# Pooled attention and two gated layers on one core: values pooled by head pairs in the first batch, a new plan of the first steps, and a denominator formed as a product with h

## The chip, the cores and the metric

The kernel runs on one core of a Trainium2 chip. The metric is device time in microseconds (us) of one launch, the median of several runs. Beside the runs stands one profiled execution, from which all rows below are taken. Engine names in rows: PE is TensorE (matmul), PEld its weight load, DVE is VectorE, ACT is ScalarE, POOL is GpSimd, SP is SyncE, which issues all DMAs of this kernel (SPq is its queue).

## The reference

```python
k_p = k.reshape(B, H, S//8, 8, D).mean(axis=3)       # B=8, H=8, S=576, D=64: 72 pooled keys
v_p = v.reshape(B, H, S//8, 8, D).mean(axis=3)
attn = softmax(scale * q @ k_p^T)                    # scale = 1/8
x = (attn @ v_p) as (4608, 512)                      # tokens x (head, d)
h = x @ w_in                                         # 512 -> 2048
P = a0 + a1*h + a2*h^2 + a3*h^3
Q = 1 + |b0|*|h| + |b1|*h^2
x = (P / (Q + 1e-6)) @ w_out                         # 2048 -> 512
out = (sigmoid(x @ w_gate) * (x @ w_val)) @ w_out2   # 512 -> 1536 -> 512
```

All of it is in 32-bit floats. The kernel splits both operands of each large product into a high and a low part, so that one product is three matmuls (`mm3`, L472).

## The kernel before

**Tiling.** The 4608 tokens are cut at the borders of batches and of 128 tokens into 40 attention tiles of 128 or 64 tokens (`token_tiles`). A block of the first layer has 512 tokens; there are nine, and each goes through 16 slices of 128 of the 2048 hidden features: 144 steps n. The four tiles of block 0 belong to batch 0; a fifth, of 64 tokens, ends that batch and opens block 1. The second layer runs after step 143, in six pairs of 384-token blocks; the change doesn't touch it.

**A step n** (loop at L759). `g1` makes h for one slice of features in a PSUM bank. `rational1`, `rational2` and `rational3` (L510 to L533) make P/Q of it: ScalarE forms Square, a scaled Abs and an affine from h, VectorE the sum u = |b1|·h² + |b0|·|h| (L517, from two SBUF tiles) and the cubic (L518, L519 with h from PSUM), ScalarE then Ln(1 + u) and Exp(-ln), the reciprocal, and VectorE corrects it and multiplies (L531 to L533). `split_g` splits the result of the step before; `g2` multiplies with w_out three steps later (LAG). In steps 0 to 15 `weights_a` also loads w_in and w_out and splits them, on ScalarE (L92, L94, L117), VectorE (L100, L118) and GpSimd (L102, L118).

**Attention** is spread over the steps by a plan (L429 to L465): a list of pieces with a step, a rank within it, and a part (0 before `split_g`, 2 behind `rational2`, 1 behind `g2`), one part for TensorE's half and one for the rest. For a tile: scores and subtraction of the maximum (L347 to L365), exponential (L371), normalisation (L378 to L382, the product on GpSimd), transposes (L389, copied by ScalarE at L393), attend (L404, copied into xs at L409 and L410). Steps -8 to -1 are the prologue (L744), in which only attention and weight conversion run; step 0 needs all of xs of block 0.

**Keys and values.** A batch's keys are pooled on VectorE in five chunks (L314) and put into a block-diagonal tile (L323). Its values come as five chunks of 128 rows (head, pooled position), are pooled on GpSimd (L331, L332) into `vp`, and 12 small DMAs (`heads_v`, L344) move them into `vh`, where the 72 pooled positions of each head start at partition 0, as the attend needs them. Batch b+1 is pooled during the steps of batch b; for batch 1 that is step -2 (keys), -1 and 0 (values).

**Order.** Each engine runs its instructions in the order of the program. Loads are issued by SyncE in the order of the plan (`units`): the first 14 into tiles that are free at the start (`early`), then three into a ring (`raw_p`), whose refill is issued when a pooling has read its slot (`done`). Five more go into named tiles in step -7.

## Time and profile before

| | us |
|---|---|
| runs, median of 3 (lowest to highest) | 1831.88 (1828.98 to 1833.6) |
| profiled execution | 1829.29 |
| its span, first to last instruction | 1827.1 |

One step of the rational in the middle of the first layer takes about 6.4 us (816.60 us for 127 steps between 173.4 and 990 us). A row of the timeline gives the start and the duration of one group of equal instructions, and in brackets the idle time of the engine ahead of it and what ended that. A table of waits gives who waited for whom: total, times, longest. TensorE's busy time is modelled at its ends, and some matmul records can be missing.

### The profile page before, as it was taken

To read this page: it belongs to the slowest core of one execution; us is meant where nothing else is said; L and a number is where in the kernel's file an instruction comes from. 1 tells how busy PE (TensorE), PEld (TensorE's weight loads), DVE (VectorE), ACT (ScalarE), POOL (GpSimd) and SP (SyncE) were. 2 spreads that over 40 slices of the span, in tenths; PEclk is the share of its full clock that TensorE was granted. 3 is DMA by queue.
4 is the path that set the end of the run, shared out by engine and by line. 5 is a ranking of instruction groups with operands and counts; after the bars stand their busy time and mean duration, and the time that the engine had idled before them with its cause. 6 is when DMAs were issued, how large, how long until landed. Compare 5 with 4: busy or idle time off the path is not lost.

```text
span 1827.1 us, 25392 instructions
## 1 busy us (share of the span) xinstructions
PE 1764.4 (97%) x9056; PEld 1523.6 (83%) x9056; DVE 1134.8 (62%) x1786; ACT 951.9 (52%) x1763; POOL 828.8 (45%) x796
## 2 busy tenths in 40 slices
PE   5699999999999999999999999999999999999999
PEld 4477877788778887788878998998998998998997
DVE  5899888888889888887886333433433333333341
ACT  4898777777777777777766222222222222222221
POOL 4767544563564555634551324334334334334241
PEclk9899999999999999999999999999999999999999
DMA  7453454443535454434465763763763763763660
GB/s 260 161 188 120 155 178 156 173 152 134 194 133 199 138 186 167 149 127 162 150 229 176 246 190 117 237 199 112 237 203 107 238 202 106 238 203 107 202 201 36
DMA packets 128973, 313.75 MB, mean 172 GB/s; under 512 B 17360, under 2 KB 49104, under 8 KB 128848
## 3 DMA queue, kind: packets, MB, share of 16 engines
q1 hardware_dynamic: 128848, 312.14, 51.1%
q8 instruction: 72, 1.18, 0.3%
q14 instruction: 53, 0.43, 0.1%
HBM read 257.95 MB, written 52.95 MB: 170 GB/s over the span
## 4 chain that ended last, share of the span: by engine, by line
PE 70%; DVE 11%; POOL 6%; ACT 5%; issue 4%; DMA 3%; SPq 1%; ACTq 0%; POOLq 0%; DVEq 0%
PE h L474 14%; PE h L476 13%; PE h L475 13%; PE acc L474 4%; PE acc L476 4%; PE acc L475 3%; PE accA L711 3%; PE accA L712 3%; PE h L712 3%; PE accA L710 3%; PE h L711 3%; PE h L710 3%; DVE u L517 2%; DVE y L519 2%; DMA w2d<-wq 1%
## 5 line engine op out<-in xcount | busy, mean ns | idle before, releaser
L647 DVE TENSOR_TENSOR t<-h,t 128x384 f32<-128x384 f32 x360 | 200.7, 557 | 388.6 <-ACT t L655 277.6
L502 POOL TENSOR_TENSOR g<-y,g 128x512 fp32r<-128x512 f32 x144 | 189.8, 1318 | 294.8 <-ACT g L499 243.8
L700 POOL TENSOR_TENSOR t<-t 128x384 f32<-128x384 f32 x72 | 84.3, 1171 | 449.1 <-issue 253.8
L474 PE MATMUL h<-xs,wi 128*128 128x512 f32 x576 | 232.4, 403 | 6.7 <-DVE xs L410 4.2
L474 PE MATMUL acc<-g,wo 128*128 128x512 f32 x576 | 232.1, 403 | 0.0
L476 PE MATMUL h<-xs,wi 128*128 128x512 f32 x576 | 227.9, 396 | 0.5 <-DVE xs L410 0.5
L475 PE MATMUL h<-xs,wi 128*128 128x512 f32 x576 | 227.4, 395 | 0.0
L476 PE MATMUL acc<-g,wo 128*128 128x512 f32 x576 | 225.3, 391 | 1.5 <-POOL g L502 1.5
L475 PE MATMUL acc<-g,wo 128*128 128x512 f32 x576 | 224.6, 390 | 0.0
L474 PE MATMUL h<-xS,wq 128*128 128x384 f32 x576 | 193.0, 335 | 0.8 <-DVE y L533 0.8
L476 PE MATMUL h<-xS,wq 128*128 128x384 f32 x576 | 193.1, 335 | 0.0
L475 PE MATMUL h<-xS,wq 128*128 128x384 f32 x576 | 192.7, 335 | 0.0
L517 DVE SCALAR_TENSOR_TENSOR u<-s,coef,u 128x512 f32<-128x512 f32 x144 | 130.3, 905 | 55.8 <-ACT u L515 54.5
L474 PE MATMUL h<-xA,wq 128*128 128x384 f32 x432 | 149.2, 345 | 0.3 <-DVE t L647 0.3
L531 DVE SCALAR_TENSOR_TENSOR y<-y,coef,h 128x512 f32<-128x512 f32 x144 | 107.2, 744 | 67.9 <-ACT h L527 65.9
L476 PE MATMUL h<-xA,wq 128*128 128x384 f32 x432 | 144.7, 335 | 0.0
L475 PE MATMUL h<-xA,wq 128*128 128x384 f32 x432 | 144.7, 335 | 0.0
L514 ACT ACTIVATE s<-h 128x512 f32<-128x512 f32 x144 | 85.1, 591 | 110.3 <-PE h L476 110.0
L474 PEld LDWEIGHTS h<-xs,wi 128*128 128x128 f32 x576 | 110.4, 192 | 32.0 <-DVE xs L410 5.3
L476 PEld LDWEIGHTS h<-xs,wi 128*128 128x128 f32 x576 | 109.9, 191 | 25.3 <-DVE xs L410 1.4
L474 PEld LDWEIGHTS acc<-g,wo 128*128 128x128 f32 x576 | 108.1, 188 | 26.1 <-issue 4.3
L476 PEld LDWEIGHTS acc<-g,wo 128*128 128x128 f32 x576 | 108.1, 188 | 25.5 <-POOL g L502 1.9
(112 smaller groups left out, 4085.2 us busy)
## 6 DMA issues: line engine op xcount, KB each, us to landing
wq<-w2d SPq DMA_DIRECT2D x252, 512.0 KB
wo<-wod SPq DMA_DIRECT2D x88, 512.0 KB
w2d<-wq SPq DMA_DIRECT2D x36, 512.0 KB
x2d<-o SPq DMA_DIRECT2D x36, 256.0 KB
out_dram<-o SPq DMA_DIRECT2D x36, 256.0 KB
raw<-in_k_dram SPq DMA_DIRECT2D x32, 256.0 KB
raw<-in_q_dram SPq DMA_DIRECT2D x32, 256.0 KB
raw<-in_v_dram SPq DMA_DIRECT2D x32, 256.0 KB
```

The lines of the kernel that those rows point to most:

```text
L474: nc.tensor.matmul(out_, wl, xh, start=start, stop=False, skip_group_check=on)
L475: nc.tensor.matmul(out_, wh, xh, start=False, stop=False, skip_group_check=on)
L476: nc.tensor.matmul(out_, wh, xl, start=False, stop=stop, skip_group_check=on)
L502: eng.tensor_tensor(out=g[:, 1], in0=y, in1=g[:, 0].bitcast(F32), op=ALU.subtract)
L514: nc.scalar.activation(s, h, AF.Square)
L517: nc.vector.scalar_tensor_tensor(out=u, in0=s, scalar=coef[:, 5:6], in1=u, op0=ALU.mult, op1=ALU.add)
L531: nc.vector.scalar_tensor_tensor(out=y, in0=y, scalar=coef[:, 0:1], in1=r, op0=ALU.add, op1=ALU.mult)
L647: nc.vector.tensor_tensor(out=out_, in0=a, in1=b, op=ALU.add)
L700: eng.tensor_tensor(out=y, in0=x, in1=y, op=ALU.mult)
L710: nc.tensor.matmul(a[t], gh, wt[:, 0], start=(f == 0), stop=False)
L711: nc.tensor.matmul(a[t], gh, wt[:, 1], start=False, stop=False)
L712: nc.tensor.matmul(a[t], gl, wt[:, 0], start=False, stop=(f == NF2 - 1))
```

## The change

Six edits:

- The values of batch 0 are loaded by pairs of heads, as 72 rows of two times 8·64, and pooled straight into `vh`: pairs 0 and 1 on GpSimd, pairs 2 and 3 on VectorE (`pool_v0`). `vp` and the 12 DMAs fall away for batch 0.
- For later batches the DMAs from `vp` to `vh` go out chunk by chunk, behind each chunk's pooling, instead of all 12 at the end.
- The fifth tile's exponential and normalisation move from steps 0 and 0 (parts 0 and 1) to the end of step -1.
- The keys of batch 1 are pooled two, two and one chunks in steps -4, -3 and -2, instead of all five in step -2.
- The second q tile is loaded behind the first instead of behind the values; the first loads are 13 instead of 14.
- The sum in Q is formed as (|b1|·|h| + |b0|)·h, with h from PSUM, and ScalarE takes its magnitude just ahead of Ln. Square falls away.

```diff
@@ -274,7 +274,7 @@
             if tag:
                 t = tag[0].tile([P, 4 * P], F32, tag=tag[1], name="raw1")
             elif start:
-                t = early([P, 4 * P], "raw0")
+                t = early([P, 8 * P if u[0] == "v" else 4 * P], "raw0")
             else:
                 t = raw_p.tile([P, 4 * P], F32, tag="raw", name="raw")
             if u[0] == "q":
@@ -284,6 +284,10 @@
             elif u[0] == "k":
                 cols = k_cols(u[2])
                 nc.sync.dma_start(t[:, :(cols.stop - cols.start) * POOL], k[u[1], :, cols.start * POOL:cols.stop * POOL])
+            elif u[1] == 0:
+
+                nc.sync.dma_start(t[:SP].rearrange("p (h x) -> p h x", h=2),
+                                  v[0][2 * u[2]:2 * u[2] + 2].rearrange("h (s j) d -> s h (j d)", j=POOL))
             else:
                 rows = v[u[1]].rearrange("h (s j) d -> (h s) (j d)", j=POOL)
                 c = u[2]
@@ -331,18 +335,31 @@
                 nc.gpsimd.tensor_tensor(out=t[:, :w], in0=t[:, :w], in1=t[:, w:2 * w], op=ALU.add)
             nc.gpsimd.tensor_tensor(out=vp[b][:m, c], in0=t[:, :D], in1=t[:, D:2 * D], op=ALU.add)
             done("v", b, c)
-
-        def heads_v(b):
-
-            vh[b] = ap1.tile([SP, H, D], F32, tag="vh", name="vh", bufs=2)
-            src = vp.pop(b)
-            for h in range(H):
-                r, end = h * SP, (h + 1) * SP
-                while r < end:
-                    c, o = divmod(r, P)
-                    m = min(end - r, P - o)
-                    nc.sync.dma_start(vh[b][r - h * SP:r - h * SP + m, h], src[o:o + m, c])
-                    r += m
+            heads_v(b, c)
+
+        def pool_v0(c):
+
+            if c == 0:
+                vh[0] = ap1.tile([SP, H, D], F32, tag="vh", name="vh", bufs=2)
+            t = take("v", 0, c)[:SP].rearrange("p (h x) -> p h x", h=2)
+            hs = slice(2 * c, 2 * c + 2)
+            if c < NJ // 2:
+                for w in (POOL // 2 * D, POOL // 4 * D):
+                    nc.gpsimd.tensor_tensor(out=t[:, :, :w], in0=t[:, :, :w], in1=t[:, :, w:2 * w], op=ALU.add)
+                nc.gpsimd.tensor_tensor(out=vh[0][:, hs], in0=t[:, :, :D], in1=t[:, :, D:2 * D], op=ALU.add)
+            else:
+                nc.vector.reduce_sum(vh[0][:, hs], t.rearrange("p h (j d) -> p h d j", d=D), axis=AX.X)
+
+        def heads_v(b, c):
+
+            if c == 0:
+                vh[b] = ap1.tile([SP, H, D], F32, tag="vh", name="vh", bufs=2)
+            r, end = c * P, min((c + 1) * P, H * SP)
+            while r < end:
+                h, s = divmod(r, SP)
+                m = min(end - r, SP - s)
+                nc.sync.dma_start(vh[b][s:s + m, h], vp[b][r - c * P:r - c * P + m, c])
+                r += m
 
         def scores(i):
             b, t0, n = tiles[i]
@@ -439,25 +456,34 @@
                 put(at[i], 2, 0, 0, a_transpose, i)
             else:
                 put(at[i] - 1, 2, 1, 1, a_transpose, i)
-            put(at[i] - 2, 3, 0, 0, exponential, i)
-            put(at[i] - 2, 3, 1, 1, normalise, i)
+            if i == n0:
+
+                put(-1, 5, 1, 1, exponential, i)
+                put(-1, 5, 1, 1, normalise, i)
+            else:
+                put(at[i] - 2, 3, 0, 0, exponential, i)
+                put(at[i] - 2, 3, 1, 1, normalise, i)
             put(at[i] - 3, 4, 1, 1, scores, i, use=[("q", i)])
         s0 = at[0]
         for c in range(NCH):
             put(s0 - 4, 0, 0, 0, ew, pool_k, 0, c, use=[("k", 0, c)])
-            put(s0 - 2, 5, 0, 0, ew, pool_v, 0, c, use=[("v", 0, c)])
+        for c in range(NJ):
+            put(s0 - 2, 5, 0, c >= NJ // 2, ew, pool_v0, c, use=[("v", 0, c)])
         put(s0 - 4, 1, 0, 0, ew, place_k, 0)
-        put(s0 - 2, 6, 0, 0, ew, heads_v, 0)
         for b in range(1, B):
             e0, e1 = max(at[first[b - 1]], -2), at[last[b - 1]]
             for c in range(2 * NCH):
                 w, f = (("k", pool_k), ("v", pool_v))[c // NCH]
                 st = e0 + c * (e1 - (3 if w == "k" else 1) - e0) // (2 * NCH)
+                if b == 1 and w == "k":
+                    st = c // 2 - 4
                 put(st, 6, 1, 1 if st < 0 else 2, ew, f, b, c % NCH, use=[(w, b, c % NCH)])
             put(e1 - 2, 3.5, 1, 1, ew, place_k, b)
-            put(e1 - 1, 7, 1, 1, ew, heads_v, b)
         plan.sort(key=lambda x: (x[0], (0, 2, 1)[x[4]], x[1], x[2]))
         units += [u for x in plan for u in x[6]]
+
+        units.remove(("q", 1))
+        units.insert(NCH + 1, ("q", 1))
         lead = plan[0][0]
         on_pe, off_pe = {}, {}
         for step, _, _, pe, rest, gen, _ in plan:
@@ -511,10 +537,10 @@
         def rational1(n):
             h = ys[n]
             s, u, y = new_tmp("s", "su", 3), new_tmp("u", "su", 3), new_tmp("y", "y", 3)
-            nc.scalar.activation(s, h, AF.Square)
-            nc.scalar.activation(u, h, AF.Abs, scale=coef[:, 4:5])
+
+            nc.scalar.activation(u, h, AF.Abs, scale=coef[:, 5:6])
             nc.scalar.activation(y, h, AF.Identity, scale=coef[:, 3:4], bias=coef[:, 2:3])
-            nc.vector.scalar_tensor_tensor(out=u, in0=s, scalar=coef[:, 5:6], in1=u, op0=ALU.mult, op1=ALU.add)
+            nc.vector.scalar_tensor_tensor(out=u, in0=u, scalar=coef[:, 4:5], in1=h, op0=ALU.add, op1=ALU.mult)
             nc.vector.tensor_tensor(out=y, in0=h, in1=y, op=ALU.mult)
             nc.vector.scalar_tensor_tensor(out=y, in0=y, scalar=coef[:, 1:2], in1=h, op0=ALU.add, op1=ALU.mult)
             ys[n] = (h, s, u, y)
@@ -522,6 +548,7 @@
         def rational2(n):
 
             h, s, u, y = ys[n]
+            nc.scalar.activation(u, u, AF.Abs)
             nc.scalar.activation(s, u, AF.Ln, scale=2.0 ** LSH, bias=ONE * 2.0 ** LSH)
 
             nc.scalar.activation(h, s, AF.Exp, scale=-1.0, bias=LSH * math.log(2.0))
@@ -726,7 +753,7 @@
                 h2(f, 0, accA[p])
 
 
-        nstart = 2 * NCH + n0
+        nstart = NCH + NJ + n0
         for i in range(nstart):
             load_unit(True)
         for i in range(RA):
```

## Rows read from the trace of the kernel before

**Rows 1.** Page, part 1: busy time of each engine, share of the span, instructions.

```profile
PE 1764.4 (97%) x9056; PEld 1523.6 (83%) x9056; DVE 1134.8 (62%) x1786; ACT 951.9 (52%) x1763; POOL 828.8 (45%) x796
```

**Rows 2.** Stage, its length, busy PE, PEld, DVE, ACT, POOL, clock, DMA share, GB/s.

```profile
27.80:41.30 13.50, 9.89 (x89) 8.20 (x89) 11.68 (x24) 12.05 (x23) 4.37 (x4) 0.88 0.87 311
44.80:173.40 128.60, 105.88 (x513) 83.24 (x512) 120.66 (x183) 111.62 (x201) 94.46 (x92) 0.89 0.49 164
173.40:990.00 816.60, 801.34 (x4072) 653.63 (x4070) 685.73 (x1083) 604.92 (x1100) 420.81 (x422) 1.00 0.46 163
```

**Rows 3.** One line's instructions, L519: duration ns min/median/max, first and last start.

```profile
L519 DVE SCALAR_TENSOR_TENSOR y<-y,coef,h x144: 746/748/750, 47.5 to 987.1; 128x512 f32<-128x512 f32 x144
```

**Rows 4.** Timeline, prologue: start, duration, engine, line, operation, count [idle before <-releaser].

```profile
8.36 1.25 POOL L331 TENSOR_TENSOR raw<-raw 128x256 f32<-128x256 f32 x2 [7.05 <-DMA raw<-in_v_dram]
11.89 2.29 PE L352 MATMUL sc<-kbd,raw 128*128 128x144 f32 x8 [1.87 <-DMA raw<-in_q_dram]
14.59 0.81 DVE L365 TENSOR_TENSOR e<-sc,mx 128x288 f32<-128x288 f32 x2
16.37 9.43 SPq L344 DMA_DIRECT2D vh<-vp  x12
16.39 1.14 POOL L382 TENSOR_TENSOR e<-e,r 128x576 f32<-128x576 f32 x1
17.58 1.92 PE L389 MATMUL pta<-ident,e 128*72 128x128 f32 x8 [3.40 <-POOL e L382]
22.40 1.60 PE L404 MATMUL psx<-aT,vh 72*64 72x128 f32 x10 [1.26 <-DMA vh<-vp]
27.13 0.66 PE L404 MATMUL psx<-aT,vh 72*64 72x128 f32 x2 [0.72 <-DMA vh<-vp]
37.56 2.78 DVE L314 TENSOR_REDUCE kp<-raw 128x64 f32<-128x512 f32 x5
40.63 0.60 ACT L409 ACTIVATE xs<-psx 128x512 fp32r<-128x512 f32 x1
```

**Rows 5.** Timeline, steps 0 to 2: first rational, fifth tile.

```profile
42.86 0.80 DVE L365 TENSOR_TENSOR e<-sc,mx 64x288 f32<-64x288 f32 x2
44.87 0.60 ACT L514 ACTIVATE s<-h 128x512 f32<-128x512 f32 x1 [0.64 <-PE h L476]
45.36 0.68 ACT L515 ACTIVATE u<-h,coef 128x512 f32<-128x512 f32 x1
57.71 1.06 PE L389 MATMUL pta<-ident,e 64*72 64x64 f32 x8 [7.44 <-POOL e L382]
59.12 0.67 ACT L117 ACTIVATE wo<-woraw 128x512 fp32r<-128x512 f32 x1 [1.41 <-POOL wo L118]
```

**Rows 6.** Groups by line, 44.8 to 173.4 us: count, busy us, mean ns, idle before.

```profile
L517 DVE SCALAR_TENSOR_TENSOR u<-s,coef,u 128x512 f32<-128x512 f32 x16 | 20.5, 1279 | 4.7 <-ACT u L515 4.6
```

**Rows 7.** Timeline, step 4: L517 beside GpSimd, and Ln behind it.

```profile
78.58 1.42 POOL L382 TENSOR_TENSOR e<-e,r 64x576 f32<-64x576 f32 x1 [1.32 <-DVE r L381]
79.05 4.00 DVE L517 SCALAR_TENSOR_TENSOR u<-s,coef,u 128x512 f32<-128x512 f32 x1
79.97 1.29 POOL L118 TENSOR_TENSOR wo<-woraw,wo 128x512 fp32r<-128x512 f32 x1
81.23 1.27 POOL L502 TENSOR_TENSOR g<-y,g 128x512 fp32r<-128x512 f32 x1
83.08 0.63 ACT L525 ACTIVATE s<-u 128x512 f32<-128x512 f32 x1 [2.88 <-DVE u L517]
```

**Rows 8.** ScalarE's waits, 44.8 to 173.4 us: total, times, longest.

```profile
ACT h L527 <- DVE y L519: 7.1, 10, 0.8
ACT s L525 <- DVE u L517: 4.9, 4, 2.9
```

**Rows 9.** TensorE's waits, 173.4 to 990 us: total, times, longest.

```profile
PE sc L352 <- ACT aT L393: 4.7, 4, 2.0
PE h L474 <- DVE xs L410: 4.2, 5, 1.5
```

## The prediction

> **What bounds the kernel now.** I read the page first. TensorE is busy 97% of the span [rows 1], so a saving on another engine counts only where TensorE waits for it. Next came the table by stage, which says where that is [rows 2]. From 173.4 to 990 us TensorE is busy 801.34 of 816.60 us: 15.3 us of waiting in 127 steps is all that can be won there. From 44.8 to 173.4 us, the sixteen steps in which the weights are still being converted, VectorE is busy 120.66 of 128.60 us and ScalarE 111.62, TensorE only 105.88, at a mean granted clock of 0.89. There the two elementwise engines set the pace. Behind 990 us no line of the change runs (L519, which the rational has in every step, starts first at 47.5 and last at 987.1 us [rows 3]). So the change is priced in three places: the prologue, the sixteen steps, and the waits left afterwards.
>
> The prologue I read from the timeline [rows 4]. GpSimd starts on the values at 8.36 us and comes to the first tile's normalisation only at 16.39, behind all five chunks. SyncE then issues twelve small copies for 9.43 us. The first attend, whose 16 matmuls start at 22.40, is drawn out by them until 27.13 + 0.66 = 27.79. From there to 41.3 us ScalarE is busy 12.05 of 13.50 us and VectorE 11.68 [rows 2]: that stretch is a chain with little air in it. It ends with the last copy into xs, 40.63 + 0.60 = 41.23 [rows 4]. What begins earlier at its front ends earlier at its back, and little else shortens it.
>
> **The change part by part. Values by head pairs.** Removed from the front: 5 chunks on GpSimd and the 12 copies. Added: 2 pairs on GpSimd, 2 on VectorE. A pair has adds of 512, 256 and 128 elements; at 1.25 us for two adds of 256 [rows 4] that is 1.25/2 x 3.5 = 2.2 us, two pairs 4.4. A q load of 256 KB now goes ahead of the values, 0.8 us at the 311 GB/s of [rows 2]; so GpSimd runs from 9.2 to 13.6 us, and the first normalisation (1.14 us) ends at 14.7 instead of 17.53. On TensorE follow the transposes (1.92), the third tile's scores (at most the 2.29 of the second's) and the attend (2.56, at 1.60 for ten): 14.7 + 1.9 + 2.1 + 2.6 = 21.3 instead of 27.8 us. VectorE's reductions of 1024 elements do not stand in the trace: the nearest row has five of 512 in 2.78 us, 0.56 each; so 1.1 each is the lower end, and 2.2, if the stride of 64 halves the rate, the upper. I take 1.1, because the reduction reads one input in either case. VectorE comes to them behind the second tile's subtraction, 14.59 + 0.81 = 15.4 [rows 4], and ends them at 17.6 us, ahead of the attend; at 2.2 the second tile's normalisation is late by 2.2. **Term: -6.5 us, between -4 and -7.5.** The second q load no longer waits behind the values (1.87 us at 11.89); that shortens nothing by itself, since the second tile waits for the first.
>
> **The second batch's keys** leave the end of the prologue (2.78 us on VectorE at 37.56) for steps -4 to -2: VectorE has the same sum in the same stretch, so nothing is booked. Their cover is the chain's remaining air, 13.50 - 11.68 = 1.8 us; without it they cost about 1.2. The twelve copies per later batch go out chunk by chunk, each behind the pooling that the refill of the ring already waits for on SyncE. For the second batch, two chunks are not in the ring: w_in and w_out loads of step -1 queue behind GpSimd there for up to 8 us. They are converted three steps of 8 us later, which covers it. Zero, and at most +2 if it does not.
>
> **The fifth tile's exponential and normalisation** move from steps 0 and 1 to step -1. In step -1 ScalarE reaches the exponential after the last copy into xs (41.23), but VectorE delivers the subtraction only at 42.86 + 0.80 = 43.66 [rows 5]: ScalarE stands 2.4 us, and its weight conversions and the first step queue behind. With the instruction's own time (0.6) less the 0.3 that ScalarE now stands before the first Square, step 0 begins 2.7 us later than it otherwise would. Given back: the exponential in step 0 (0.6) and some of a wait there (0.3), and in step 1 the 1.41 us that ScalarE waits for GpSimd's wo [rows 5], which sits behind that tile's normalisation, with 0.4 of another wait: 2.7 in all. **Term: 0, between +2.7 and -2.** TensorE's wait of 7.44 us for that tile [rows 5] goes too. I book nothing for it: it lies behind the h of step 2, for which ScalarE has conversions queued in front, so ScalarE is late next.
>
> **The denominator, VectorE.** L517 read two SBUF tensors; now it reads one from SBUF and h from PSUM, the form of L519. In the sixteen steps L517 cost 20.5 us [rows 6]; at L519's 0.748 [rows 3] it is 12.0, so 8.5 us go. Where they sat is seen in step 4 [rows 7]: L517 took 4.00 us, from 79.05 to 83.05, while GpSimd worked from 78.58 to 82.50 without a break, and Ln stood 2.88 us for it. L519 took 746 to 750 ns in all 144 cases [rows 3], whatever GpSimd did.
>
> The Trainium skill (SBUF — State Buffer, section "SBUF: two separate sides") says that VectorE with two SBUF inputs and GpSimd take an exclusive lock for one instruction, the other being blocked. The trace agrees on who is blocked; on how long it differs, three GpSimd instructions and not one. By one instruction the stall in step 4 would be at most 1.42 us and the saving 1.8 us smaller.
>
> **The denominator, ScalarE.** Square goes (0.49 from its start to the next one's [rows 5]); an Abs comes, SBUF to SBUF, between L517 and Ln. Its price lies between nothing, where ScalarE stood waiting, and 0.63 (Ln's duration, same operands [rows 7]) less 0.49: +0.15 a step, 2.4 over sixteen. In the path from L517 to Exp it costs nothing. Ln was ready 0.8 us before L519 let Exp go (7.1 us in ten waits [rows 8]); the Abs fits into that, and L517 itself starts 0.49 earlier. So a step paced by VectorE shrinks by its stall and up to 0.5 us, and one paced by ScalarE grows by 0.15. Waits of ScalarE on these two, 7.1 + 4.9 = 12.0 us [rows 8], are the most that can go; less 2.4 and what steps 0 and 1 already had (1), about -8. Some stalls move on to the next VectorE instructions that read SBUF alone, L100 and L118, and TensorE binds some of the last steps. **Term: -4, between +2.4 and -8.**
>
> **Afterwards.** ScalarE's copies of the transposes and VectorE's L410 stand behind rational1 in each step; both come 0.5 us earlier where ScalarE waits for h. TensorE waits 4.7 us for the first and 4.2 us for the second [rows 9], in nine events of up to 2.0 us. 0.5 from each is 4.5 us. **Term: -4.5, between 0 and -8** (8 is half of the 15.3).
>
> **The sum.** The profiled execution took 1829.3 us: 1827.1 of span and 2.2 around it. -6.5 + 0 - 4 - 4.5 = -15, so 1814.3. The runs' median, 1831.9, lies 2.6 above; I predict runs and add it: 1817.
>
> **The rivals.** (a) The start alone gains: ScalarE, 87% busy in the sixteen steps [rows 2], takes over the pace as soon as VectorE lets go, and the later waits stay. -6.5 + 2 = -4.5: 1827. For it speaks how close the two engines stand; against it Ln's wait of 2.88 us, in which ScalarE had nothing else to do.
> (b) The start gains nothing: the values or the weights come late, or ScalarE's stand of 2.4 us is not given back, -8.5: 1823. The Trainium skill speaks for this (DMA: Bandwidth & Descriptors, section "Why a DMA increments its semaphore by 16 and not by 1"): a transfer uses the largest number of engines up to 16 that divides both outer dimensions, so 72 rows get 12 and 128 get 16. No row of the trace tells the engines of a transfer. By rows alone, 1.18 MB of values at 311 GB/s are 3.8 us, a third more is 5.1; the last pair then lands at about 14 us, and VectorE reaches it at 16.5. Only if it were three times as slow would the attend feel it.
> (c) All of it: start -7.5, steps -8, later waits -8: 1808. For it speaks that L517's whole excess is waiting.
> (d) Slower: the Abs stands in ScalarE's chain in all 144 steps. If ScalarE set the pace after 173 us too, 128 x 0.15 = 19 us and 2.4 before, less the start's 6.5: +15, 1847. It decides from where ScalarE's work in a step passes TensorE's. The row has 604.92 us of ScalarE beside 801.34 of TensorE [rows 2], so a third more work would be needed; the Abs adds 3%.
>
> **How the numbers follow.** Forecast 0.50, (a) 0.20, (b) 0.10, (c) 0.15, (d) 0.05. The forecast's own spread is 1811 to 1823. The range from 1808 to 1828 takes in (a) and (b), (c) in half, and leaves out (d) with what lies beyond either end. A measurement of this kernel can tell about 0.3%, 5.5 us, from no change: faster means below 1826.4. The forecast, (b), (c) and a fourth of (a) lie there: 0.80. The rest of (a) is the same, 0.15; (d) is slower, 0.05.
>
> **What would show it.** Right: no copies from vp ahead of the first attend, which ends near 21 us; the last copy into xs near 35; L517 at 0.75 us everywhere; the sixteen steps, 128.6 us from first to last, near 124; TensorE's waits for aT and xs about halved. Wrong: the first step of the rational begins later than 42 us (the exponential's stand is not covered); L100 and L118 grow by what L517 loses; or ScalarE without gaps in steps that had them.

## The result, and the profile of the changed kernel

| | before | after |
|---|---|---|
| median of four runs, us | 1831.56 (1828.98 to 1833.6) | 1813.45 (1809.41 to 1815.3) |
| ratio, 95% interval | | 0.9898 [0.9885, 0.9910] |
| profiled execution, us | 1829.29 | 1815.3 |
| its span, us | 1827.1 | 1813.5 |

The change saves 18.1 us of the median. The profiled execution of after is the slowest of its four runs and shows 13.6 us of it. A second profile of the same kernel, taken beside the last experiments (called *after again*: 1810.7 us, ratio 0.9884 [0.9868, 0.9900], span 1809.0), shows 18.1. Both are read below.

After, the rational's lines are L541 (Abs of h), L542 (Identity), L543 (the new product with h, formerly L517), L544 and L545 (formerly L518 and L519), L551 (Abs of the product), L552 (Ln), L554 (Exp) and L558 to L560. L421 is the attend, L426 and L427 the copies into xs, L410 those into aT, L528 the last product into g.

First the page's part 1, to be laid beside [rows 1], and the table by stage, to be laid beside [rows 2]. Its columns are the stretch and its length, then busy us and instructions of each engine, the mean granted clock, the DMA share and GB/s. The second stretch is the sixteen steps, the third goes as far as [rows 2] does.

```profile
PE 1761.6 (97%) x9056; PEld 1525.1 (84%) x9056; DVE 1104.0 (61%) x1788; ACT 975.8 (54%) x1763; POOL 801.3 (44%) x787
...
24.00:38.50 14.50, 12.03 (x91) 9.74 (x89) 11.93 (x27) 12.02 (x22) 6.56 (x7) 0.70 1.01 319
44.35:163.85 119.50, 100.36 (x500) 79.90 (x499) 107.43 (x178) 112.83 (x198) 89.41 (x92) 0.90 0.54 176
163.85:976.40 812.55, 801.66 (x4069) 654.71 (x4068) 663.54 (x1085) 626.79 (x1100) 400.39 (x422) 1.00 0.48 164
```

The sixteen steps took 128.60 us and take 119.50; VectorE gave up 13 us of work there and ScalarE, at 112.83 of 119.50, is now the busiest engine. From there to 976 us TensorE does the work of [rows 2]'s last stretch in 812.55 instead of 816.60 us. The stretch between the prologue's first attend and its last copy into xs (24.0 to 38.5 us) is 14.5 us long, 1.0 longer than before. ScalarE is as busy in it as before (12.02 us), and TensorE's granted clock is 0.70 there instead of 0.88; whether that costs the 1.0 us was not tested.

Where the time went, step by step: the start of ScalarE's first instruction of a step, in us.

```
step          0       1       2       4       5       8      16      72     143
before    44.87   53.10   61.92   77.87   88.42  112.95  172.89  540.69  983.63
after     44.35   52.75   60.26   75.99   83.50  106.66  163.85  529.84  970.05
again     42.91   51.33   58.84   74.95   82.50  105.70  162.87  525.76  965.52
```

So the start gave 0.5 us (again: 2.0), the sixteen steps 8.5 (8.1), and the steps from 16 to 143 4.5 (8.1). Both profiles are of one kernel, and the 3.6 us by which they differ in the last stretch are TensorE's clock. The same 3.3 us in the first and in the second profile:

```profile
282.50:285.80 3.30, 3.30 (x9) 2.53 (x9) 2.60 (x5) 3.24 (x7) 1.84 (x2) 0.50 0.84 306
...
282.50:285.80 3.30, 3.30 (x16) 2.72 (x15) 2.60 (x5) 3.24 (x7) 1.30 (x1) 1.00 0.73 285
```

TensorE is busy all the time in both, but at a granted clock of 0.50 (1.2 GHz) it does 9 matmuls and at 1.00 (2.4 GHz) 16. Ahead of it, from 255 to 283 us, it had waited 2.1 us in the first profile and 1.9 in the second. In steps 16 to 143 the first profile has 6.8 us at 1.2 GHz, in which 3.4 us of work are lost, and the second none; the kernel before has 3.4 us and loses 1.7. With that loss taken off (an estimate: half of the time at 1.2 GHz), these steps take 809.0 us before and 802.8 (again: 802.6) after, 6.2 to 6.4 us less. Six more profiles below have the same rational, and they lie between 801.8 and 803.2 us counted so.

Step 4, in which L517 stood for 4.00 us [rows 7], shows where the sixteen steps gain. The timeline of that step in after (start, duration, engine, line, operation; in brackets the idle time before it and what ended it):

```profile
75.99 0.67 ACT L541 ACTIVATE u<-h,coef 128x512 f32<-128x512 f32 x1
76.05 1.42 POOL L399 TENSOR_TENSOR e<-e,r 64x576 f32<-64x576 f32 x1 [1.31 <-DVE r L398]
76.56 0.76 ACT L542 ACTIVATE y<-h,coef 128x512 f32<-128x512 f32 x1
...
77.35 0.75 DVE L543 SCALAR_TENSOR_TENSOR u<-u,coef,h 128x512 f32<-128x512 f32 x1 [0.89 <-ACT y L542]
77.44 1.32 POOL L118 TENSOR_TENSOR wo<-woraw,wo 128x512 fp32r<-128x512 f32 x1
...
78.13 0.64 ACT L551 ACTIVATE u<-u 128x512 f32<-128x512 f32 x1 [0.29 <-DVE u L543]
78.71 1.29 POOL L528 TENSOR_TENSOR g<-y,g 128x512 fp32r<-128x512 f32 x1
78.73 0.75 DVE L545 SCALAR_TENSOR_TENSOR y<-y,coef,h 128x512 f32<-128x512 f32 x1
78.80 0.63 ACT L552 ACTIVATE s<-u 128x512 f32<-128x512 f32 x1
```

GpSimd works without a break beside it, as before, and the product takes 0.75 us all the same. The product over all steps, with shortest, median and longest duration in ns, and in the line below it over the sixteen steps alone:

```profile
L543 DVE SCALAR_TENSOR_TENSOR u<-u,coef,h x144: 694/747/749, 45.7 to 972.1; 128x512 f32<-128x512 f32 x144
...
L543 DVE SCALAR_TENSOR_TENSOR u<-u,coef,h x16: 735/747/748, 45.7 to 158.4; 128x512 f32<-128x512 f32 x16
```

That is the duration of [rows 3] in every case, where [rows 6] has a mean of 1279. What ScalarE waits for in the sixteen steps (us in total, times, longest) is next; its waits for the product and for y (L545) are 2.6 us beside 12.0 in [rows 8]. Behind it stands what TensorE waits for afterwards (163.9 to 976.4 us), beside [rows 9]:

```profile
ACT u L551 <- DVE u L543: 2.4, 6, 0.8
ACT u L541 <- PE h L502: 2.1, 2, 1.4
ACT h L554 <- DVE y L545: 0.2, 1, 0.2
...
PE psx L421 <- DVE y L560: 6.3, 6, 1.4
PE h L500 <- DVE xs L427: 2.0, 3, 1.3
PE acc L502 <- POOL g L528: 1.3, 1, 1.3
PE sc L369 <- ACT aT L410: 1.2, 2, 0.8
```

The prologue, in order of time. These are the lines that answer to [rows 4]:

```profile
12.81 2.06 POOL L348 TENSOR_TENSOR raw<-raw 72x512 f32<-72x512 f32 x2 [11.51 <-DMA raw<-in_v_dram]
14.95 0.45 POOL L349 TENSOR_TENSOR vh<-raw 72x128 f32<-72x128 f32 x1
...
16.58 3.71 DVE L351 TENSOR_REDUCE vh<-raw 72x128 f32<-72x1024 f32 x2
17.91 1.15 POOL L399 TENSOR_TENSOR e<-e,r 128x576 f32<-128x576 f32 x1
19.11 1.92 PE L406 MATMUL pta<-ident,e 128*72 128x128 f32 x8 [5.63 <-POOL e L399]
...
22.89 1.15 PE L421 MATMUL psx<-aT,vh 72*64 72x128 f32 x16
37.87 0.58 ACT L426 ACTIVATE xs<-psx 128x512 fp32r<-128x512 f32 x1
40.65 0.69 ACT L388 ACTIVATE e<-e 64x576 f32<-64x576 f32 x1 [2.21 <-DVE e L382]
```

The twelve copies are gone from the attend's way. But the first pair of values lands at 12.81 us (again: 10.69), not at 9.2; a pair takes 2.5 us of GpSimd, not 2.2; a reduction 1.89, not 1.1. The attend ends at 24.04 (again: 22.66) instead of 27.79, the last copy into xs at 38.45 (37.00) instead of 41.23. ScalarE then stands for the fifth tile, 2.21 us, before it comes to the weights and to step 0.

### The profile page after: what moved, and what is told of

Its sections match the earlier page's. It is cut to its first block, busy times and chain, and to the rows that moved or that the text cites. A ratio compares the mean times of both kernels' runs of the same rounds, so it can differ in the third digit from the quotient of the medians.

```text
span 1813.5 us, 25319 instructions
## 1 busy us (share of the span) xinstructions
PE 1761.6 (97%) x9056; PEld 1525.1 (84%) x9056; DVE 1104.0 (61%) x1788; ACT 975.8 (54%) x1763; POOL 801.3 (44%) x787
## 3 DMA queue, kind: packets, MB, share of 16 engines
q8 instruction: 72, 1.18, 0.3%
## 5 line engine op out<-in xcount | busy, mean ns | idle before, releaser
L528 POOL TENSOR_TENSOR g<-y,g 128x512 fp32r<-128x512 f32 x144 | 187.2, 1300 | 283.8 <-ACT g L525 216.6
L541 ACT ACTIVATE u<-h,coef 128x512 f32<-128x512 f32 x144 | 98.2, 682 | 104.7 <-PE h L502 104.4
L558 DVE SCALAR_TENSOR_TENSOR y<-y,coef,h 128x512 f32<-128x512 f32 x144 | 107.4, 746 | 75.2 <-ACT h L554 73.0
L543 DVE SCALAR_TENSOR_TENSOR u<-u,coef,h 128x512 f32<-128x512 f32 x144 | 106.4, 739 | 70.9 <-ACT y L542 70.3
```

The lines of the kernel that those rows point to most:

```text
L528: eng.tensor_tensor(out=g[:, 1], in0=y, in1=g[:, 0].bitcast(F32), op=ALU.subtract)
L541: nc.scalar.activation(u, h, AF.Abs, scale=coef[:, 5:6])
L543: nc.vector.scalar_tensor_tensor(out=u, in0=u, scalar=coef[:, 4:5], in1=h, op0=ALU.add, op1=ALU.mult)
L558: nc.vector.scalar_tensor_tensor(out=y, in0=y, scalar=coef[:, 0:1], in1=r, op0=ALU.add, op1=ALU.mult)
```

## The experiments

Ratios are to the kernel before, each with its 95% interval. The changed kernel has 0.9898 and, again, 0.9884; their mean, 0.9891, is what differences to it are taken from. 0.001 is 1.83 us.

### One half of the change at a time

The kernel before with the rational's change alone:

```diff
-            nc.scalar.activation(s, h, AF.Square)
-            nc.scalar.activation(u, h, AF.Abs, scale=coef[:, 4:5])
+            nc.scalar.activation(u, h, AF.Abs, scale=coef[:, 5:6])
...
-            nc.vector.scalar_tensor_tensor(out=u, in0=s, scalar=coef[:, 5:6], in1=u, op0=ALU.mult, op1=ALU.add)
+            nc.vector.scalar_tensor_tensor(out=u, in0=u, scalar=coef[:, 4:5], in1=h, op0=ALU.add, op1=ALU.mult)
...
+            nc.scalar.activation(u, u, AF.Abs)
```

> The kernel before with the rational's change alone: L517 reads u from SBUF and h from PSUM, Square falls away, Abs ahead of Ln; the start is as before. Theory A (the trace of the changed kernel: step 0 begins 0.5 us earlier, step 2 1.7, step 16 9.0, step 143 13.6): nearly all comes from the rational, so about -12 us, 1820 (sixteen steps near 120 us, L517 at 0.75 us). Theory B, the forecast's terms: -4 in the sixteen steps and -4.5 later, 1823, and the rest belongs to the start. Theory C: the sixteen steps are shorter only because the fifth tile's work left steps 0 and 1; then they stay above 125 us here and the time is about 1826.

Measured: 1814.25 us, 0.9907 [0.9893, 0.9922], so -17.0. The sixteen steps take 120.1 us (45.85 to 165.99), steps 16 to 143 801.8 against 810.7 before.

The changed kernel with the old rational (the same lines reversed):

> The changed kernel with the rational of before (Square, L517 from two SBUF tiles, no Abs ahead of Ln): the new start alone. Theory A: 1 to 2 us faster than before, 1830, since in the changed kernel's trace step 2 begins only 1.7 us earlier. Theory B: 6.5 us faster, 1825. Theory C: the start and the rational need each other (TensorE's wait of 7.4 us for the fifth tile counts once ScalarE is faster), so this one is no faster and x1 falls short of -12.

Measured: 1828.68 us, 0.9987 [0.9974, 0.9999], so -2.5, and between -0.2 and -4.8. The sixteen steps take 128.0 us, as before. Its profile is that of the slowest of its ten runs, and in it step 16 begins only 0.5 us earlier than before (172.36), so where the 2.5 us of the median lie is not shown. The two add up to the whole: the rational's lines carry seven eighths of the gain, the start's the rest.

### Why the start gave so little: the loads

The load of a pair in two pieces, 64 rows and 8:

```diff
-                nc.sync.dma_start(t[:SP].rearrange("p (h x) -> p h x", h=2),
-                                  v[0][2 * u[2]:2 * u[2] + 2].rearrange("h (s j) d -> s h (j d)", j=POOL))
+                vs = v[0][2 * u[2]:2 * u[2] + 2].rearrange("h (s j) d -> s h (j d)", j=POOL)
+                for lo, hi in ((0, 64), (64, SP)):
+                    nc.sync.dma_start(t[lo:hi].rearrange("p (h x) -> p h x", h=2), vs[lo:hi])
```

> The changed kernel with each load of a head pair cut in two, 64 rows and 8 rows, same bytes and places. In the trace of the changed kernel the transfers move 232 to 243 GB/s from 10 to 16 us, before 222 to 389, and the first pair lands at 12.8 us instead of the 9.2 of the forecast. Theory A: too few DMA engines take part in a transfer of 72 rows; 64 rows use all, the first pair lands by 10.5 us, the first attend ends 2 us earlier, 1 to 2 us gained. Rival B: the rows end in the first 72 partitions whichever engine brings them, so the rate stays near 235 GB/s and nothing is gained; eight issues instead of four cost up to 1 us.

The same bytes into all 128 rows, half the pooling left out:

```diff
-                nc.sync.dma_start(t[:SP].rearrange("p (h x) -> p h x", h=2),
-                                  v[0][2 * u[2]:2 * u[2] + 2].rearrange("h (s j) d -> s h (j d)", j=POOL))
+                nc.sync.dma_start(t[:, :2 * S * D // P], v[0][2 * u[2]:2 * u[2] + 2].rearrange("h s d -> (h s d)").rearrange("(p x) -> p x", p=P))
```

> Leaves out half of the pooling of the first batch's values, and the values used are wrong: each head pair's bytes are loaded as they lie in memory into 128 rows of 576 elements instead of 72 rows of 1024, and the pooling takes the first half of 72 of them. Only the first 20 us are read from it. Theory A (the rows 0 to 71 limit the transfer): 300 GB/s or more from 10 to 16 us (changed kernel 232 to 243, rational alone with the old loads 304), the first pair lands by 10.5 us. Theory B (what is loaded when, not where to): the rate stays at 230 to 265 GB/s.

Measured: 1810.82 us, 0.9888 [0.9873, 0.9903] for the first; 1808.87 in a single run of the second, which leaves work out and whose time is not compared. What tells them apart is the rate while the values come in. First the same row (its last number is GB/s) of before, of the changed kernel and of the load in two pieces, from 10 to 16 us. In the run with 128 rows the values come in earlier, so the last two rows have the changed kernel and that run from 8 to 10 us:

```profile
10.00:16.00 6.00, 2.31 (x9) 1.94 (x8) 3.95 (x10) 1.25 (x2) 5.45 (x12) 1.00 0.96 310
...
10.00:16.00 6.00, 3.48 (x16) 3.26 (x16) 3.53 (x10) 0.68 (x1) 3.03 (x4) 1.00 1.02 236
...
10.00:16.00 6.00, 2.73 (x14) 2.51 (x12) 4.33 (x12) 0.79 (x2) 3.81 (x5) 0.96 1.01 239
...
8.00:10.00 2.00, 0.18 (x1) 0.21 (x2) 0.44 (x2) 0.69 (x3) 0.00 (x0) 1.00 0.88 174
...
8.00:10.00 2.00, 1.54 (x6) 1.57 (x7) 0.55 (x3) 0.69 (x3) 0.19 (x1) 1.00 0.99 381
```

The DMA engines are busy in all of them (0.88 to 1.02); at 236 GB/s they move less. Two pieces change nothing (239). 128 rows bring the rate back (381). So it is the rows that are written, 0 to 71, that hold the values up, and not how the transfer is cut. (Nor is it the length of a contiguous piece: 2 KB of a row in the kernel before, 2 KB in the changed one.) How much of the first pair's lateness this is, is not shown: with 128 rows it lands at 9.81 us in the one run, and with the 72-row load at 10.08 to 12.81 in nine profiles.

The Trainium skill (SBUF — State Buffer, section "Door 1: the DMA port swizzle (why `[64,N]` ≈ `[32,N]`)") has partitions reach sixteen ports by bits of their number, and partitions 0 to 63 only eight of them. An estimate by that page's 436 GB/s for sixteen is 218 for eight and, with 64 of 72 rows through them, 245; the trace's 236 and 239 lie near it, though other loads share their stretch. The other rule of the Trainium skill, which the prediction weighed (DMA: Bandwidth & Descriptors, section "Why a DMA increments its semaphore by 16 and not by 1"), gives 64 rows all sixteen engines; the trace, 239 GB/s with 64 and 8, speaks against it as the cause here.

### Why the start gave so little: the fifth tile and the keys

The fifth tile's exponential and normalisation back in step 0:

```diff
-            if i == n0:
-
-                put(-1, 5, 1, 1, exponential, i)
-                put(-1, 5, 1, 1, normalise, i)
-            else:
-                put(at[i] - 2, 3, 0, 0, exponential, i)
-                put(at[i] - 2, 3, 1, 1, normalise, i)
+            put(at[i] - 2, 3, 0, 0, exponential, i)
+            put(at[i] - 2, 3, 1, 1, normalise, i)
```

> The changed kernel with the fifth tile's exponential and normalisation back in step 0. Theory A: ScalarE no longer stands 2.2 us for the subtraction in step -1, so step 0 begins about 2.7 us earlier than in the changed kernel (near 41.6 us); given back in step 0 (0.6) and by GpSimd in step 1 (up to 1.4): between -1 and +1 against the changed kernel. Rival: TensorE's wait for that tile's transposes (7.4 us before) is what the move took away and it counts: 3 to 6 us slower than the changed kernel.

Measured: 1812.32 us, 0.9893 [0.9876, 0.9909]. From the last copy into xs to step 0 it takes 4.05 us (35.93 to 39.98), in the changed kernel 5.9 in both profiles: the move does make step 0 about 1.9 us later. From step 0 to step 2 it takes 15.92 us, the changed kernel 15.91, the kernel with the rational alone 15.88, the kernel before 17.05: with the new rational the move gives nothing back there. (With the old rational the new start does shorten these steps, from 17.05 to 16.17.) Step 16 begins at 160.46 us, 2.4 and 3.4 earlier than in the two profiles of the changed kernel; its last copy into xs came 1.1 and 2.5 earlier. In the medians no difference can be told.

Both together, the tile back and the load in two pieces:

> The changed kernel with two of the edits tried before together: the fifth tile's exponential and normalisation back in step 0, and the head pairs loaded in 64 and 8 rows. Theory A: the first alone takes 1.7 us from the time between the last copy into xs and step 0 (4.0 us there instead of 5.8) and gives nothing back, so 1 to 3 us faster than the changed kernel, 1811. Theory B: both are noise, the same as the changed kernel within 1 us.

Measured: 1810.58 us, 0.9878 [0.9864, 0.9892]. The last copy into xs ends at 38.20 us, step 0 begins 3.54 later and step 16 at 160.88. On the same chip the changed kernel itself was run again:

> The changed kernel once more, beside the two others on the same chip. 1811 to 1815 us by every theory; its profile tells how much the landing of the first values varies from run to run (12.81 us in its first profile, 10.08 to 11.95 in other kernels with the same loads).

Measured: 1810.7 us, 0.9884 [0.9868, 0.9900]. The two are the same; neither piece of the start is worth anything that the medians show.

The second batch's keys all in step -2, as before:

```diff
-                if b == 1 and w == "k":
-                    st = c // 2 - 4
```

> The changed kernel with the second batch's keys pooled in step -2 again, all five chunks. The forecast booked nothing for this edit, with about 1.2 us if the chain has no air. Theory A: within 1.5 us of the changed kernel, 1812 to 1815. Rival: the five reductions (2.8 us) stand ahead of the last copies into xs again and delay step 0 by 2 us or more, 1816.

Measured: 1812.69 us, 0.9891 [0.9869, 0.9913]: the same as the changed kernel within some 4 us. That allows the term of zero and does not prove it; step 0 begins at 43.47 us, between the two profiles of the changed kernel, so the rival's delay is not seen.

### What in the rational gains: Square, the operand, the Abs

The changed kernel with Square put back at the head of the step, its result unused:

```diff
+            nc.scalar.activation(s, h, AF.Square)
             nc.scalar.activation(u, h, AF.Abs, scale=coef[:, 5:6])
```

> The changed kernel with Square put back in front of rational1, its result unused: VectorE's product still reads one SBUF tensor and h from PSUM, ScalarE has one instruction more in every step and everything behind it 0.49 us later, as in the kernel before. Theory A (ScalarE paces the sixteen steps once VectorE is free of the wait on GpSimd: it is busy 112.83 of 119.50 us in the changed kernel): 16 x 0.49 = 8 us there, and the 4.5 us later are lost again, about +12, 1825. Theory B (the gain is the port's alone): the sixteen steps stay within 3 us of the changed kernel's 119.5, later waits the same, 1815 to 1817.

Measured: 1836.27 us, 1.0018 [1.0008, 1.0027]: 23 us slower than the changed kernel, and slower than the kernel before. The sixteen steps grow to 126.9 us (+7.4), steps 16 to 143 to 820.8 (806.2 and 802.7 in the two profiles of the changed kernel), and to 817.3 with the loss at 1.2 GHz taken off (802.8 and 802.6).

The same kernel with that first instruction as a copy of h that the product reads, so that it has two SBUF operands again:

```diff
-            nc.scalar.activation(s, h, AF.Square)
+            nc.scalar.activation(s, h, AF.Copy)
...
-            nc.vector.scalar_tensor_tensor(out=u, in0=u, scalar=coef[:, 4:5], in1=h, op0=ALU.add, op1=ALU.mult)
+            nc.vector.scalar_tensor_tensor(out=u, in0=u, scalar=coef[:, 4:5], in1=s, op0=ALU.add, op1=ALU.mult)
```

> As the run with Square kept, but ScalarE's extra instruction is a copy of h into SBUF and VectorE's product reads that copy: two SBUF tensors again, the same number of instructions on every engine. The two runs differ in the operand alone. Theory A: the product is again stretched beside GpSimd (mean over 1.1 us in the sixteen steps instead of 0.74), 2 to 8 us slower than the run with Square kept. Theory B (ScalarE hides it): within 2 us of that run, though the product is stretched.

Measured: 1841.19 us, 1.0052 [1.0036, 1.0069]: 6 us above the one before it, between 3 and 10 by the two intervals. The product's line (shortest, median, longest in ns):

```profile
L544 DVE SCALAR_TENSOR_TENSOR u<-u,coef,s x144: 693/751/3360, 43.0 to 1000.5; 128x512 f32<-128x512 f32 x144
```

The stalls are back (3360 at the most), with the same instructions on every engine, and the run is 6 us slower in all. Its profile, the slowest of its four runs, takes 829.1 us for steps 16 to 143, but with 23.9 us at 1.2 GHz (Square kept: 6.8); with the loss taken off it is 817.2, the same as with Square kept. So in these profiles the operand's price after the sixteen steps is all in the clock; TensorE's longest wait for aT is 3.6 us here and 1.9 there. The operand, by which the gain was to come, is a third of the rational's 17.

The changed kernel without the Abs of the product:

```diff
-            nc.scalar.activation(u, u, AF.Abs)
-            nc.scalar.activation(s, u, AF.Ln, scale=2.0 ** LSH, bias=ONE * 2.0 ** LSH)
+            nc.scalar.activation(s, u, AF.Ln, scale=2.0 ** -40, bias=ONE * 2.0 ** LSH)
```

> The changed kernel without its new last step of the denominator: the Abs of the product is left out and the logarithm reads the product itself, scaled down so that its argument stays positive; the reciprocal of the denominator is therefore not computed. What is measured is the price of one ScalarE instruction between the product and the logarithm. Theory A (the runs so far add up: the head's Square 22, the second SBUF operand 6, and the Abs about 10 us of loss, which is what is left to the measured -17): this kernel is about 10 us faster than the changed one, a ratio to the kernel before of 0.983 to 0.985. Theory B (the Abs hides where ScalarE would wait for VectorE's y in any case, as the prediction says; the 10 us in the sum are only the two other prices not adding up): same time as the changed kernel, 0.988 to 0.990, with ScalarE's waits at the exponential for y grown by what the Abs took, from 0.2 us in the sixteen steps to some 8.

Measured: 1805.93 us, 0.986 [0.9843, 0.9876]: 5.7 us faster than the changed kernel, between the two theories. In the sixteen steps theory B holds. ScalarE's waits there in this kernel:

```profile
ACT h L553 <- DVE y L545: 9.7, 16, 0.8
ACT u L541 <- PE h L502: 3.0, 2, 1.8
ACT s L551 <- DVE u L543: 2.5, 6, 0.8
```

Where the Abs is gone the exponential waits for y in each of the sixteen steps, 9.7 us, and the steps are only 1.2 us shorter (118.3). The Abs does hide there. Afterwards it does not: steps 16 to 143 take 798.3 us, none of it at 1.2 GHz, 4 us less than the 802.6 to 802.8 with the Abs.

From 173 to 990 us, TensorE's work in the same 817 us says what each instruction costs. The rows of the kernel before, the changed kernel, Square kept, and no Abs:

```profile
173.00:990.00 817.00, 801.74 (x4074) 653.95 (x4072) 686.06 (x1085) 605.32 (x1100) 420.81 (x422) 1.00 0.46 163
...
173.00:990.00 817.00, 806.11 (x4095) 659.43 (x4094) 660.47 (x1079) 625.90 (x1099) 397.22 (x420) 1.00 0.48 163
...
173.00:990.00 817.00, 793.72 (x4018) 644.11 (x4017) 654.65 (x1071) 679.84 (x1216) 396.75 (x420) 1.00 0.47 161
...
173.00:990.00 817.00, 809.62 (x4139) 664.75 (x4137) 663.58 (x1087) 547.93 (x976) 402.47 (x425) 1.00 0.48 166
```

And what TensorE waits for in that stretch with Square kept:

```profile
PE psx L421 <- DVE y L561: 6.8, 7, 1.4
PE h L500 <- DVE xs L427: 6.1, 5, 1.9
PE sc L369 <- ACT aT L410: 5.2, 5, 1.9
PE h L500 <- DVE y L561: 2.2, 2, 1.8
```

With Square the waits for xs and aT are back, a little above where they stood before [rows 9], with all else as in the changed kernel: it is Square's absence that takes them from 11.3 us to 3.2. ScalarE is busy 679.84 of 817 us there, so its load alone isn't the bound; an instruction of about the same length, the Abs, costs a fourth of it in its other place. What VectorE's idle time ahead of the product ended with, over all steps of the changed kernel (us, times), says what stands behind the head:

```profile
  ACT y L542: 70.3, 81
```

In 81 of 144 steps VectorE had nothing to do until Identity was done. The product does not use Identity's result; both read h from PSUM. The same line for the product of the kernel before, of Square kept and of the run with two SBUF operands:

```profile
  ACT u L515: 54.5, 63
...
  ACT y L543: 93.0, 91
...
  ACT u L542: 45.9, 54
```

With two SBUF operands it starts behind the Abs, with h from PSUM behind Identity. In step 4 that is 1.36 us behind the step's first instruction (75.99 and 77.35), where before it was 1.18 (77.87 and 79.05), although Square is gone. So the two runs above differ in more than the stalls: the 6 us are the price of the stalls less what the earlier start is worth, and neither was measured alone. What makes the product wait for Identity was not tested. An instruction ahead of Identity delays VectorE in those steps; one behind the product doesn't.

### The magnitude on VectorE instead

```diff
             nc.vector.scalar_tensor_tensor(out=u, in0=u, scalar=coef[:, 4:5], in1=h, op0=ALU.add, op1=ALU.mult)
+            nc.vector.tensor_scalar(out=u.bitcast(I32), in0=u.bitcast(I32), scalar1=0x7fffffff, scalar2=None, op0=ALU.bitwise_and)
...
-            nc.scalar.activation(u, u, AF.Abs)
```

> The changed kernel with the magnitude ahead of Ln taken by VectorE (the sign bit cleared in place, SBUF to SBUF, directly behind its product) instead of ScalarE. From the runs so far: Square's removal is worth about 22 us, one SBUF operand less about 6, and the Abs costs about 10. Theory A (ScalarE's place in the step is what counts: each instruction there moves the copies that TensorE waits for): 5 to 10 us faster than the changed kernel, 1804 to 1808. Theory B (an operation of VectorE from SBUF to SBUF waits for GpSimd as L517 did, and VectorE passes 85% after the sixteen steps): same as the changed kernel or up to 8 us slower, with durations of several us beside GpSimd's runs.

Measured: 1872.99 us, 1.0219 [1.0205, 1.0234], 60 us above the changed kernel; neither theory has it. The mask's line, ScalarE's waits from 44 to 1030 us, and the engines from 180 to 1030:

```profile
L544 DVE TENSOR_SCALAR u<-u x144: 426/428/4020, 44.2 to 1031.6; 128x512 int32<-128x512 int32 x144
...
ACT s L552 <- DVE u L544: 129.2, 110, 5.0
ACT h L554 <- DVE y L546: 106.0, 143, 0.8
ACT u L541 <- PE h L502: 57.2, 44, 3.2
...
180.00:1030.00 850.00, 804.79 (x4022) 649.56 (x4021) 734.39 (x1197) 543.89 (x963) 406.65 (x418) 0.99 0.45 155
```

The mask reads and writes SBUF alone and takes 0.43 us, but up to 4.02 when GpSimd works; over 144 cases its mean is 733 ns, so the stalls are 0.3 x 144 = 44 us of its 106. VectorE is 86% busy, TensorE 95%. Now the exponential waits for y in 143 of 144 steps, since the mask stands ahead of L545 too. How much of the 60 us its own time costs and how much its stalls was not separated.

## Why the prediction was right, point by point

The total (1817 forecast; 1813.45) came out, in part by luck, by terms that missed in opposite directions.

**The start: -6.5 forecast, -2.5 measured** (nearer to zero than its bound of -4). The sum's first line failed by the loads: "GpSimd runs from 9.2 to 13.6 us" has 72 rows land as fast as 128, and they get 236 GB/s where the stretch had 310. The first pair landed 1.5 to 3.6 us late. The reductions took 1.89 us each where I took 1.1. The bounds of 1.1 and 2.2 were misread: the five reductions in [rows 4] are four of 512 elements and one of 256, and one of 512 takes 0.67 us (L314, median), so they should have been 1.3 and 2.7. The pairs took 2.5 us for 2.2. With these the attend ended 3.8 to 5.1 us earlier instead of 6.5, and 1.0 (0.9) of that was gone by the last copy into xs. Rival (b) had the mechanism (values late) and its rows' price, but for another reason, and its "only if it were three times as slow" counted VectorE's pairs and not the first one, on GpSimd, behind which the normalisation queues.

**The fifth tile: 0.** The stand of 2.4 us was there (2.21 us), and step 0 began at 44.35 and 42.91, which the prediction had named as a sign that it is not covered. The delay was 1.9 us (2.4 by the run with both edits), not 2.7; ScalarE's stand before the first Square is 0.64 us in [rows 5], not 0.3. With the new rational nothing was given back in steps 0 and 1, and in the two profiles without the move step 16 begins 2.0 to 3.4 us earlier (160.46 and 160.88 against 162.87 and 163.85). So the profiles put the term nearer to its bound of +2.7 than to zero. The medians can't tell the two apart; the zero is not refuted, its reason is.

**The keys and SyncE's copies: 0.** The keys' zero fits, within some 4 us. (The 1.2 us that they were to cost without air follow from no row.) The copies for later batches were not tried alone.

**The sixteen steps: -4 forecast, -8.5 and -8.1 in the two profiles**, at the far bound. The stall of L517 went as told, 8.6 us of it (20.5 to 11.9). But it did not start 0.49 us earlier: it now waits for Identity, and VectorE's idle time ahead of it grew from 4.7 us [rows 6] to 9.1. The term that was mis-sized is ScalarE's: Square for Abs was priced by their durations, +0.15 a step. Square alone is worth 7.4 us there, the Abs 1.2. The fear that stalls move on to L100 and L118 did not come true: L118 takes 12.0 us in the sixteen steps, before 11.8, and L100 18.0, before 20.6. That ScalarE takes over the pace (rival (a)) is half true: it is the busiest engine now and waits 2.6 us for VectorE's two results instead of 12.0, but by then 8 us are gained.

**Afterwards: -4.5 forecast, -4.5 and -8.1 in the two profiles, about -6.3 with the loss at 1.2 GHz taken off.** That the first profile has just the forecast's 4.5 is chance: it lost 3.4 us to the clock, the kernel before 1.7, and the prediction has no term for that. The mechanism, copies into aT and xs earlier by Square's 0.5 us, is the one that the run with Square kept shows. Its size was read from nine waits of two tiles. These fell by 5.7 us, from 8.9 to 3.2, but TensorE's wait for y at the attend (L421, 6.3 us above) grew from what it was before:

```profile
PE psx L404 <- DVE y L533: 2.9, 5, 0.9
```

What the Abs costs there, 4 us, was not booked at all.

**The rational as a whole** can be walked through in single steps from the changed kernel with the old rational: the Abs added, with the operands left as they were, 0.9987 to 1.0052, +12 us; one operand from PSUM, 1.0052 to 1.0018, -6; the head's instruction removed, 1.0018 to 0.9891, -23. So the edit that I priced as a swap of two durations carries most of the gain, and the one that I argued from is a third of it. The Abs costs 12 us behind a long head (8 to 16 by the intervals) and 5.7 behind a short one (2 to 9); with the loss at 1.2 GHz taken off the profiles have 8 and 6, so that the two differ is not shown. The other steps may depend on their order as well, which was not tried. Rival (d), in which one more ScalarE instruction in each step decides, is right about what Square costs (0.16 us a step over 144) and wrong about where the Abs stands.

## What to carry to other kernels

Price an instruction by its place: 0.49 us at the head of a step, ahead of all that the step computes, was worth 23 us over 144 steps, though its engine was 83% busy with it; 0.63 us beside another engine's chain was worth 6; 0.43 us in VectorE's chain between product and exponential, 0.73 with its stalls, cost 60. Before a load is reshaped, read the rate of a load into the same rows, not the rate of the queue. Before a few us between two profiles are put down to an edit, set apart the time that TensorE spent at the lower clock: here it was all of the 3.6 us by which two profiles of one kernel differ after step 16. When a new start gains less than it should, look at the first arrival and walk down the chain to the first compute step: here of 6.5 us there were left 5.1 at the attend, 4.2 at the last copy and 2.0 at the first step, in the better of the two profiles.

## What the runs showed of the hardware

- While loads into 72 rows (0 to 71) came in, 236 GB/s were moved (10 to 16 us), with the DMA engines busy throughout; cut at row 64 it was 239. With the same bytes into 128 rows it was 381 (8 to 10 us, when the changed kernel had 174).
- A VectorE reduction over 1024 elements with a stride of 64 takes 1.89 us, 1.8 ns an element; over 512 contiguous ones (L314) it takes 0.67 us in the median, 1.3 ns an element.
- A VectorE instruction that reads and writes SBUF alone, 0.43 us by itself, took up to 4.02 us beside GpSimd; the product with an operand from PSUM never took more than 0.75. That product started behind Identity, which reads the same h, and with two SBUF operands behind the Abs ahead of it (70.3 us of idle time in 81 steps, and 45.9 in 54).
- On ScalarE, Abs and Identity of one h, which do not depend on each other, start 0.57 us apart, though the Abs takes 0.67 (75.99 and 76.56 in step 4); the Ln that needs the Abs starts 0.67 behind it (78.13 and 78.80), after its 0.64.
- In one profile TensorE ran 3.3 us at a granted clock of 0.50 (9 matmuls) and in a second profile of the same kernel at 1.00 (16 matmuls), with the same steps ahead of it and waits of 2.1 and 1.9 us in that. What decides between the two was not tested.
